# New planner durations, and a task order refined with 320 more seeds and engine pins, in a fused attention and ResMLP kernel

## The chip, the cores and the metric

The kernel runs on one core of a Trainium2 chip. The core has a matrix engine (PE, with its weight loads shown apart as PEld), a vector engine (DVE), a scalar engine (ACT), GpSimd (POOL) and a sync engine (SP), which here only issues DMAs. Each engine executes its own instructions in the order in which the program gives them, and waits on semaphores for the others. The metric is the device time of one execution in microseconds (us), the median of several runs. Beside it stands one profiled execution, whose trace gives every instruction's start and duration.

## The reference

Everything that is computed, cut to its core (B = 4 batches, 8 heads, S = 768 positions, head width 64, model width 512, hidden width 2048, 4 sink positions, a window of 128):

```python
scores = scale * q @ k.T                       # per batch and head, 768 x 768
keep = is_sink | ((rel >= 0) & (rel < window)) # 4 sinks, and the last 128 positions
a = exp(where(keep, scores, -1e9) - max); a = a / (sum(a) + 1e-9)
x = (a @ v), heads side by side                # batch, 768, 512
tok = einsum('ts,bsd->btd', w_tok, alpha1 * x + beta1)
u = x + lam * tok
ch = maximum((alpha2 * u + beta2) @ w_ch1, 0) @ w_ch2
out = u + lam * ch
```

Inputs and output are float32; the kernel multiplies in float16 and sums in float32.

## The kernel before, in words

Rows are cut into 6 tiles of 128. For each batch the stages are: load q, k and v and cast them to float16; transpose q and k (batches 0 and 1 on PE, batches 2 and 3 by a transposing DMA, L630); scores S of a key tile against two query tiles (L719 adds the mask as a bias by matmul in batch 0, L724 and L788 multiply q by k); exp on ACT into E (L746); masking of E by a multiply on DVE (L761) or two selects on POOL (L686); the sinks (L656, L661); the product with v (pv, L818 and L825) and its normalisation on DVE (L850, L851); the scaled copy xh (L860, or `mul` and `plus`, L869 and L872); mixing over tokens on PE (tok, L956), its addition on DVE (L963) and a cast (u, L356 or L358); the transpose of u (uTp on PE in batch 0, L997; a transposing DMA, L1015, afterwards); the affine step on it, uT (L980 on ACT, L982 on DVE); the first MLP product h (L1036: 512 matmuls over the four batches) with its relu (L1042 ACT, L1044 DVE); and the second MLP product. That last one is plain in batch 0 (ch, L1221). In batches 1 to 3 it is one Strassen step: seven products P1 to P7 (L1153) of sums of h halves (`h_sums`, L1094 to L1097) and differences of weight halves (`w2_sums`, L1068), added into the rows by L1166, L1184, L1189 and L1192.

The order of the work is not written by hand. Each piece is a task (`add`) with a priority, the engines on which it may run with a duration in ns for each, the tasks that it needs and the buffers that it takes. `Plan.run` simulates the five engines, the buffers and the DMA rings with these durations: again and again it takes, of the tasks that are ready, the one that can start first on the engine on which it would end first, priority breaking ties. It knows one resource that two engines share: a POOL task and a DVE task marked `port=True` never run at once in the plan. `uTx` does not mark its affine step so. A change of the PE's array shape (`mode`) costs 95 ns in the plan. `Plan.emit` then writes the instructions in the order in which the plan starts them. Before it does, it shakes the priorities: `TURNS` is a list of 30 seeds, each of which adds Gaussian noise to some priorities (`shuffle`). So the durations and the seeds settle two things and nothing else: the order of instructions in each engine's queue, and the engine of each task that has a choice. On the chip, every instruction still starts when the semaphores that it waits for allow.

Where the plan foresees that PE is idle before 36 us, it emits dummy matmuls on a zero tile (L349) that keep PE busy. They compute nothing that is used.

Buffers limit how far the order can be moved: four PSUM buffers of one bank for all products (`d`), two of two banks for the scores (`S`), six for E, twelve for the rows x, two for hT.

Of the kernel before, what the change touches and what calls it, by code (L numbers as in the profile page):

```python
# [10 lines left out]
FP16 = mybir.dt.float16  # L11
# [4 lines left out]
PE, ACT, DVE, POOL, SP = "pe", "act", "dve", "pool", "sp"  # L16
# [95 lines left out]
class Plan:  # L112
# [9 lines left out]
    def add(self, prio, engs, fn, after=(), uses=(), mode=None, lands=None, port=False,  # L122
            since=0.0):


        t = Task(len(self.tasks), prio, engs, fn, after, uses, mode, lands, port, since)
        for a in t.needs:
            a.then.append(t)
        self.tasks.append(t)
        return t  # L130

    def run(self, prio):

        tasks = self.tasks
        rank = [0] * len(tasks)
# [32 lines left out]
        def pick():  # L168
            best = None
            spare = {k: sorted(h for h, x in zip(homes[k], busy[k]) if not x) for k in homes}  # L170
            for r, i in open_:
                at = ready[i]
                if best is not None and at > best[0]:
                    continue
                t = tasks[i]
                asked = {}
                for b in t.uses:
                    if b.home is None:
                        asked[b.kind] = asked.get(b.kind, 0) + 1
                if any(len(spare[k]) < n for k, n in asked.items()):  # L180
                    continue
                at = max([at] + [spare[k][n - 1] for k, n in asked.items()])
                own = None
                for e in t.engs:
                    at_e = max(free[e], at)
                    if e == POOL or (e == DVE and t.port):
                        at_e = max(at_e, port)
                    key = (at_e + FW * t.engs[e], at_e, r, at_e + t.engs[e], i, e)
                    if own is None or key < own:
                        own = key  # L190
                if best is None or own[1:] < best:
                    best = own[1:]
            return best
# [49 lines left out]
        self.ends = free  # L243
        return steps

    def emit(self, turns):

        prio = [t.prio for t in self.tasks]
        for seed in turns:
            prio = shuffle(prio, seed)  # L250
        for t, e, start, stop, idle in self.run(prio):
            t.at = (e, start, stop)
            if idle:
                self.fill[1](self.pools["d"][0].tile(
                    [128, 512], FP32, tag=f"d_{idle[0]}", bufs=1, name=f"idle{t.i}"), idle[1])
            for b in t.uses:
                if b.t is None:
                    pool, shape, dtype = self.pools[b.kind]
                    b.t = pool.tile(b.shape or shape, b.dtype or dtype,
                                    tag=f"{b.kind}_{b.home}", bufs=1, name=b.name)  # L260
            t.fn(e)


def shuffle(prio, seed):
# [15 lines left out]
def kernel(  # L280
# [125 lines left out]
    w1f = const.tile([P, NC, DFF], FP16, name="w1f")  # L406
    w2f = const.tile([P, NF, DM], FP16, name="w2f")

    gates = sb.tile([1, 32], FP16, tag="pt_1", bufs=1, name="gates")

    STRASSEN = (1, 2, 3)
    GATES = (1, 2, 3)
# [2 lines left out]
    PAIRS = 3  # L415

    TURNS = (13523, 134113, 50022, 128275, 136711, 187603, 125671, 100730, 14946, 163131, 178432, 158827, 183776, 137680, 153375, 26742, 367527, 307353, 376563, 212018, 255075, 397706, 218147, 375675, 393913, 224567, 207692, 352780, 243076, 346008)
    W1_SINCE = 20000.0

    V0 = (((0, 1), (2, 3), (4, 5)), ((0, 1, 2), (3, 4, 5)))  # L420
# [269 lines left out]
    def scores(p, b, j, Gs, bias=False):  # L690
# [51 lines left out]
        for G, hps, n, pS, eT in units:  # L742
            done["S", b, j, G] = a

            def ex(e, n=n, pS=pS, eT=eT):
                nc.scalar.activation(  # L746
                    eT.t, pS.t[:, :, 0 : n * w].rearrange("p e (i w) -> p e i w", i=n),
                    AF.Exp, scale=scale)

            x_ = add(p + 0.1, {ACT: 170 + 2 * n * w * 0.835}, ex, [a], [pS, eT])  # L750
            if not bias:
                def mk(e, eT=eT):
                    if e == POOL:
                        ev = eT.t.rearrange("p e i w -> p (e i) w")
                        keep(ev[:, :, 0:P], 0, 1, -1)
                        if w > P:
                            keep(ev[:, :, P:w], -1, -1, 1)
                        return
                    m = mask0 if j == 0 else (maskn if j < NR - 1 else maskn[:, :, 0:P])
                    ev = eT.t.rearrange("p e i w -> p (e i) w")  # L760
                    nc.vector.tensor_mul(ev, ev, m.to_broadcast(list(ev.shape)))  # L761

                c = {DVE: 60 + 2 * n * w * 0.66}
                if b and j:
                    c[POOL] = 2 * (150 + n * w * 0.9)
                x_ = add(p + 0.2, c, mk, [x_], [eT], port=True)
            for g in (0, 1) if G is None else (G,):
                off = 2 * g if G is None else 0
                E[b, j, g] = (eT, off)
                done["E", b, j, g] = [x_]  # L770
# [38 lines left out]
    def pv(p, b, r, G):  # L809
# [46 lines left out]
        if b == 0:  # L856
            c = slice(256 * G, 256 * G + 256)

            def half(e):
                engine[e].tensor_mul(  # L860
                    bh.t[:, c], bx.t.rearrange("p h d -> p (h d)")[:, c], la1_b[:, c])

            done["xh", b, r, G] = add(
                p + 0.3, {POOL: 730}, half, [a, done["la1"]], [bx, bh], port=True)
        elif G == 1:
            bt = Buf("tm", None, None, f"tm{b}_{r}")

            def mul(e):
                engine[e].tensor_mul(bt.t, bx.t.rearrange("p h d -> p (h d)"), la1_b)  # L869

            def plus(e):
                engine[e].tensor_add(bh.t, bt.t, lb1_b)  # L872

            a = add(p + 0.3, {POOL: 1350}, mul, [a, done["x", b, r, 0], done["la1"]], [bx, bt], port=True)
            done["xh", b, r, 1] = add(
                p + 0.4, {POOL: 1390, DVE: 690}, plus, [a, done["lb1b"]] + prior, [bh, bt], port=True)
            done["xb", b, r] = None
# [55 lines left out]
    def cast_w2(p, i):  # L933
        for a in range(4 * i, 4 * i + 4):
            src = wst[f"w2_{a - a % 2}"]
            done["w2", a] = add(
                p, {DVE: 980, POOL: 1400},
                lambda e, a=a, src=src: engine[e].tensor_mul(w2f[:, a, :], src.t[:, a % 2, :], lam_b),
                [done["wst", f"w2_{a - a % 2}"], done["lam"]], [src], port=True)

# [68 lines left out]
    def uTx(p, b, ti):  # L1009

        if (b, 0) not in uT:
            uT[b, 0] = Buf("uT", None, None, f"uT{b}")
        bo, bu = uT[b, 0], u16[b, ti]
        done["uTd", b, ti] = add(
            p, {SP: 1220}, lambda e: nc.sync.dma_start_transpose(  # L1015
                bo.t[:, :, ti * P : (ti + 1) * P], bu.t),
            [done["u16", b, ti]], [bu, bo], lands=(6, 100))
        if ti % 3 < 2:
            return
        chk = ti // 3  # L1020
        for c in range(NC):
            o = (c, slice(chk * NTOK, (chk + 1) * NTOK))
            done["uT", b, chk, c] = add(
                p + 0.1 + 0.01 * c, {DVE: 380, ACT: 700},
                lambda e, c=c, o=o: affine(e, bo.t[:, o[0], o[1]], bo.t[:, o[0], o[1]], c),
                [done["uTd", b, 3 * chk + i] for i in range(3)] + [done["ab2"]], [bo])

# [29 lines left out]
    def w2_sums(p):  # L1057

        for g in range(HF // 2):
# [5 lines left out]
            def sub(o, i0, i1, after, n_):  # L1065
                def f_(e, bw=bw):
                    ab = [w2f[:, x_[0], x_[1]] if isinstance(x_, tuple) else bw.t[:, x_] for x_ in (o, i0, i1)]
                    engine[e].tensor_sub(*ab)  # L1068
                return add(p + 4 * g + n_, {DVE: 420, POOL: 1400}, f_, after, [bw], port=True)

            a1 = sub(0, (f, hi_), (f, lo_), ws, 0)
            a3 = sub((f, hi_), (k_, hi_), (f, hi_), wk + [a1] + [done.get(("ch", 0, ti)) for ti in range(NR)], 1)
# [5 lines left out]
    def h_sums(p, b, what):  # L1078
# [11 lines left out]
        for g in range(2):  # L1090
# [16 lines left out]
                after = [done["S2", b, g]] + [done["P2", b, n_] for n_ in range(3)]  # L1107
            uses = {"S3": [h0, h1, hs[g]], "S1": [h1], "S2": [h0, h1], "S4": [h0]}[what]
            uses = uses + ([own[g]] if own and what in ("S2", "S4") else [])
            done[what, b, g] = add(p + 0.1 * g, {DVE: 880}, made, after, uses, port=True)  # L1110

    hS = {}
    hS2 = {}
# [3 lines left out]
    def prod(p, b, what, nt):  # L1117
# [46 lines left out]
        def plus(p, bx, cols, more):  # L1164
            def f_(e):
                nc.vector.tensor_add(row(bx)[:, cols], row(bx)[:, cols], pc.t)  # L1166
            u_ = done["u16", b, nt if bx is top else nt + 3]
            return add(p, {DVE: 400}, f_, [a, u_] + more, [pc, bx])

        def store(p, bx, ti, cols, after):  # L1170
            n_ = (cols.stop - cols.start) // 64
# [10 lines left out]
        elif what == "P6":  # L1182
            def u2(e):
                nc.vector.tensor_add(bt.t, bt.t, pc.t)  # L1184

            u = add(p + 0.1, {DVE: 400}, u2, [a, done["read", b, "P1", nt]], [pc, bt])

            def ot(e):
                engine[e].tensor_add(row(top)[:, hi_], row(top)[:, hi_], bt.t)  # L1189
# [3 lines left out]
                    row(bot).rearrange("p (a d) -> p a d", a=2), row(bot).rearrange("p (a d) -> p a d", a=2),  # L1193
                    bt.t.unsqueeze(1).to_broadcast([P, 2, HD]))

            done["U12", b, nt] = add(p + 0.3, {POOL: 760, DVE: 400}, ot, [u, done["u16", b, nt]], [bt, top], port=True)
            done["U2", b, nt] = add(
                p + 0.2, {POOL: 1300, DVE: 690}, ob,
                [u, done["u16", b, nt + 3], done["O21", b, nt]], [bt, bot], port=True)
# [191 lines left out]
                else:  # L1391
                    pv(p, nb, *args)

    plan.emit(TURNS)


# [33 lines left out]
```

The softmax here doesn't subtract the row's maximum and nothing guards it: scores larger than these inputs give would overflow.

## Time and profile before

| what | us |
|---|---|
| median of 3 runs (lowest and highest) | 256.96 (256.52 to 257.1) |
| the profiled execution's own time | 257.06 |
| its span, first to last instruction | 255.3 |
| PE busy, of which dummy matmuls (L349, 106 of them) | 247.4, 9.4 |
| DVE, ACT, POOL busy | 190.0, 142.6, 88.3 |

The span is 1.76 us shorter than the time of its execution; what lies outside it is start and end of the program. A matmul's end is modelled in this profile: a row such as "L1036 ... x512, 326 ns mean" counts about 0.16 us after the next matmul has begun. So PE's busy time hides gaps of up to some 0.2 us, and how dense PE runs is better read from the time between the starts of matmuls. A group of the profile is one line of code on one engine with its busy time, mean duration, and the idle time of its engine just before it, with the work that ended that idle time.

### The profile page before, as it was taken

To read this page: it belongs to the slowest core of one execution; us is meant where nothing else is said; L and a number is where in the kernel's file an instruction comes from. 1 tells how busy PE (TensorE), PEld (TensorE's weight loads), DVE (VectorE), ACT (ScalarE), POOL (GpSimd) and SP (SyncE) were. 2 spreads that over 40 slices of the span, in tenths; PEclk is the share of its full clock that TensorE was granted. 3 is DMA by queue.
4 is the path that set the end of the run, shared out by engine and by line. 5 is a ranking of instruction groups with operands and counts; after the bars stand their busy time and mean duration, and the time that the engine had idled before them with its cause. 6 is when DMAs were issued, how large, how long until landed. Compare 5 with 4: busy or idle time off the path is not lost.

```text
span 255.3 us, 5519 instructions
## 1 busy us (share of the span) xinstructions
PE 247.4 (97%) x2174; PEld 160.9 (63%) x2174; DVE 190.0 (74%) x402; ACT 142.6 (56%) x236; POOL 88.3 (35%) x108
## 2 busy tenths in 40 slices
PE   8999998999999999899999999999999999999994
PEld 7754645675555544456678676558668666667883
DVE  6777998696878878578889997877789764136782
ACT  2689845989848035688971225867571125775000
POOL 7409802344445330159653460735310101000000
PEclk9999999999999999999999999999999999999999
DMA  6998999999943998599778689501000156000105
GB/s 202 195 223 292 216 230 392 373 370 218 218 73 115 186 260 190 117 205 220 155 138 182 125 191 251 85 3 21 3 0 3 59 167 146 0 0 3 63 4 185
DMA packets 86130, 38.80 MB, mean 152 GB/s; under 512 B 73540, under 2 KB 80460, under 8 KB 86104
## 3 DMA queue, kind: packets, MB, share of 16 engines
q1 hardware_dynamic: 82320, 35.14, 56.5%
q0 software_dynamic: 3744, 3.28, 8.1%
q8 instruction: 17, 0.28, 0.5%
q14 instruction: 9, 0.07, 0.1%
q10 hardware_dynamic: 40, 0.03, 0.0%
HBM read 29.91 MB, written 6.29 MB: 142 GB/s over the span
## 4 chain that ended last, share of the span: by engine, by line
PE 88%; DMA 4%; DVE 3%; POOL 1%; issue 1%; ACT 1%; POOLq 0%; ACTq 0%
PE h L1036 33%; PE P L1153 21%; PE tok L956 11%; PE ch L1221 8%; PE pv L825 5%; PE S L724 4%; DMA n<-in_q_dram 4%; DVE uT L982 1%; PE S L719 1%; PE tp L614 1%; PE pv L818 1%; POOL n L497 1%; PE wT L916 1%; ACT uT L980 1%; DVE w2f L1068 1%
## 5 line engine op out<-in xcount | busy, mean ns | idle before, releaser
L1036 PE MATMUL h<-uT,w1f 128*128 128x384 f16 x512 | 91.9, 326 | 2.7 <-DVE uT L982 1.3
L1036 PEld LDWEIGHTS <-w1f 128*128 128x128 f16 x512 | 47.3, 98 | 34.5 <-issue 5.5
L1042 ACT ACTIVATE hT<-h 128x384 f16<-128x384 f32 x99 | 48.3, 492 | 26.1 <-PE h L1036 25.6
L1153 PEld LDWEIGHTS <-hT 128*128 128x128 f16 x408 | 39.8, 98 | 6.7
L746 ACT ACTIVATE E<-S 128x1024 f16<-128x1024 f32 (+1 forms) x39 | 37.9, 1001 | 7.5 <-PE S L724 3.7
L869 POOL TENSOR_TENSOR tm<-x,la_b 128x512 f32<-128x512 f32 x18 | 26.2, 1454 | 26.3 <-DVE xh L872 19.1
L956 PE MATMUL tok<-xh,wtokT 128*128 128x512 f16 x144 | 33.4, 379 | 0.0
L356 ACT CAST u<-x 128x512 f16<-128x512 f32 x19 | 11.7, 618 | 31.2 <-DVE x L963 31.1
L1153 PE MATMUL P<-w2f,hT 128*128 128x256 f16 x216 | 25.9, 273 | 0.0
L1166 DVE TENSOR_TENSOR x<-x,P 128x256 f32<-128x256 f32 x45 | 18.3, 418 | 8.2 <-PE P L1153 7.9
L1044 DVE TENSOR_SCALAR hT<-h 128x384 f16<-128x384 f32 x29 | 15.8, 553 | 10.9 <-PE h L1036 10.5
L956 PEld LDWEIGHTS <-wtokT 128*128 128x128 f16 x144 | 14.0, 98 | 14.6
L1221 PE MATMUL ch<-w2f,hT 128*128 128x512 f16 x96 | 23.0, 379 | 0.0
L1153 PE MATMUL P<-w2s,hT 128*128 128x256 f16 x192 | 22.8, 273 | 0.0
L851 DVE TENSOR_TENSOR x<-pv,rec 128x256 f32<-128x256 f32 x48 | 20.4, 424 | 1.7
L358 POOL CAST vfs<-vnat 128x512 f16<-128x512 f32 x18 | 15.0, 840 | 16.2 <-DMA vnat<-in_v_dram 16.0
L963 DVE TENSOR_TENSOR x<-x,tok 128x512 f32<-128x512 f32 x24 | 16.2, 684 | 5.7 <-PE tok L956 5.7
L356 ACT CAST n<-nat 128x768 f16<-128x768 f32 x16 | 13.2, 829 | 10.8 <-DMA nat<-in_q_dram 8.8
L825 PEld LDWEIGHTS <-E 128*128 128x128 f16 x328 | 15.2, 97 | 6.0 <-issue 1.6
L825 PE MATMUL pv<-vfs,E 128*128 128x65 f16 x328 | 17.9, 194 | 0.0
L358 POOL CAST u<-x 128x512 f16<-128x512 f32 x5 | 3.1, 621 | 34.8 <-DVE x L963 21.1
L1221 PEld LDWEIGHTS <-hT 128*128 128x128 f16 x96 | 8.6, 98 | 9.1 <-issue 0.2
(131 smaller groups left out, 327.4 us busy)
## 6 DMA issues: line engine op xcount, KB each, us to landing
out_dram<-x SPq DMA_DIRECT2D x21, 256.0 KB, 2.8
nat<-in_q_dram SPq DMA_DIRECT2D x13, 384.0 KB, 5.3
nat<-in_k_dram SPq DMA_DIRECT2D x13, 384.0 KB, 5.7
vnat<-in_v_dram SPq DMA_DIRECT2D x18, 256.0 KB, 5.2
wst_w<-in_moe_w_ch_dram SPq DMA_DIRECT2D x8, 512.0 KB, 7.4
wtn<-in_moe_w_tok_dram SPq DMA_DIRECT2D x6, 384.0 KB, 4.7
w1f<-in_moe_w_ch_dram POOLq DMA_DIRECT2D x4, 512.0 KB, 11.1
v<-in_v_dram SPq DMA_DIRECT2D x12, 128.0 KB, 6.4
```

The source lines that it names most:

```text
L356: nc.scalar.copy(o, i)
L358: engine[e].tensor_copy(o, i)
L746: nc.scalar.activation(eT.t, pS.t[:, :, 0 : n * w].rearrange("p e (i w) -> p e i w", i=n), AF.Exp, scale=scale)
L825: nc.tensor.matmul(po.t[:, hl, :], eT.t[:, e_, off + i, c : c + P], vf[j][:, h, :], start=(r < 2 and n == 0), stop=(n == len(parts) - 1 an ...
L851: nc.vector.tensor_mul(bx.t[:, 4 * G : 4 * G + 4, :], po.t[:, :, 0:D], rec.t.to_broadcast([P, 4, D]))
L869: engine[e].tensor_mul(bt.t, bx.t.rearrange("p h d -> p (h d)"), la1_b)
L956: nc.tensor.matmul(pt.t, wtokT[:, si, ti * P : (ti + 1) * P], hs[si].t, start=(si == 0), stop=(si == NR - 1))
L1036: nc.tensor.matmul(ph.t, w1f[:, c, fi * P : (fi + 1) * P], bu.t[:, c, chk * NTOK : (chk + 1) * NTOK], start=(c == 0), stop=(c == NC - 1))
L1042: nc.scalar.activation(bh.t[:, fi, :], ph.t, AF.Relu)
L1153: nc.tensor.matmul(pc.t, hh[:, nt * P : (nt + 1) * P], w(fi), start=(first and n_ == 0), stop=(n_ == HF - 1), skip_group_check=True)
L1166: nc.vector.tensor_add(row(bx)[:, cols], row(bx)[:, cols], pc.t)
L1221: nc.tensor.matmul(pc.t, bh.t[:, fi, nt * P : (nt + 1) * P], w2f[:, fi, :], start=(fi == 0), stop=(fi == NF - 1))
```

## The change

Three things change, and all matmuls, additions, casts and DMAs stay what they are.

First, durations. Nine entries of the planner's tables get other numbers; in the order of the diff they are those of the mask of E (on POOL), tm (`mul`), the scaling of w2f (L938), the affine step uT of batches 1 to 3, `w2_sums`, `h_sums`, the additions L1166 and L1184, and U12 (L1189). Second, order. `emit` takes a second list, `NUDGES`, of 320 seeds, applied to the priorities after `TURNS`. Each seed does one of six things, chosen by a hash: move one priority, move a few, move a run of 2 to 25 neighbours together, swap two, pin one task to the first or second engine of its list (or free it), or move one and pin another. Read from the hash alone, 111 seeds swap, 108 move a run of neighbours, 57 move a few, 11 move one, 10 pin and 23 move and pin. `run` honours a pin by trying no other engine for that task. Third, the 64-byte tile `gates`, into which three tiny DMAs write so that later loads wait for the weights of h, gets its own memory; before, it shared that of the first `pt` buffer.

```diff
-    def run(self, prio):
+    def run(self, prio, pin=None):
...
-                for e in t.engs:
+                one = pin[i] if pin and pin[i] <= len(t.engs) else 0
+                for n, e in enumerate(t.engs):
+                    if one and n + 1 != one:
+                        continue
...
-    def emit(self, turns):
+    def emit(self, turns, nudges):
         prio = [t.prio for t in self.tasks]
         for seed in turns:
             prio = shuffle(prio, seed)
-        for t, e, start, stop, idle in self.run(prio):
+        pin = [0] * len(prio)
+        for seed in nudges:
+            nudge(prio, pin, seed)
+        for t, e, start, stop, idle in self.run(prio, pin):
...
+def nudge(prio, pin, seed):
+    n, x, wide = len(prio), seed, (0.5, 1, 2, 4, 8, 16, 32, 64)
...
+    kind = mix() % 6
+    w = wide[mix() % 8]
+    c = mix() % n
...
+    if kind == 0:
+        prio[c] += by()
+    elif kind == 1:
+        for _ in range(2 + mix() % 5):
+            i = (c + mix() % 60) % n
+            prio[i] += by()
+    elif kind == 2:
+        m = 2 + mix() % 24
+        y = by()
+        for i in range(c, min(c + m, n)):
+            prio[i] += y
+    elif kind == 3:
+        i = (c + 1 + mix() % 80) % n
+        prio[c], prio[i] = prio[i], prio[c]
+    elif kind == 4:
+        pin[c] = mix() % 3
+    else:
+        prio[c] += by()
+        i = (c + mix() % 30) % n
+        pin[i] = mix() % 3
...
-    gates = sb.tile([1, 32], FP16, tag="pt_1", bufs=1, name="gates")
+    gates = const.tile([1, 32], FP16, name="gates")
...
+    NUDGES = (45552149, 788903931, 542345562, 549274876,
...
-                    c[POOL] = 2 * (150 + n * w * 0.9)
+                    c[POOL] = 2 * (190 + n * w * 1.03)
...
-            a = add(p + 0.3, {POOL: 1350}, mul, [a, done["x", b, r, 0], done["la1"]], [bx, bt], port=True)
+            a = add(p + 0.3, {POOL: 1440}, mul, [a, done["x", b, r, 0], done["la1"]], [bx, bt], port=True)
...
-                p, {DVE: 980, POOL: 1400},
+                p, {DVE: 850, POOL: 1450},
...
-                p + 0.1 + 0.01 * c, {DVE: 380, ACT: 700},
+                p + 0.1 + 0.01 * c, {DVE: 450, ACT: 700},
...
-                return add(p + 4 * g + n_, {DVE: 420, POOL: 1400}, f_, after, [bw], port=True)
+                return add(p + 4 * g + n_, {DVE: 490, POOL: 1400}, f_, after, [bw], port=True)
...
-            done[what, b, g] = add(p + 0.1 * g, {DVE: 880}, made, after, uses, port=True)
+            done[what, b, g] = add(p + 0.1 * g, {DVE: 970}, made, after, uses, port=True)
...
-            return add(p, {DVE: 400}, f_, [a, u_] + more, [pc, bx])
+            return add(p, {DVE: 425}, f_, [a, u_] + more, [pc, bx])
...
-            u = add(p + 0.1, {DVE: 400}, u2, [a, done["read", b, "P1", nt]], [pc, bt])
+            u = add(p + 0.1, {DVE: 425}, u2, [a, done["read", b, "P1", nt]], [pc, bt])
...
-            done["U12", b, nt] = add(p + 0.3, {POOL: 760, DVE: 400}, ot, [u, done["u16", b, nt]], [bt, top], port=True)
+            done["U12", b, nt] = add(p + 0.3, {POOL: 1260, DVE: 425}, ot, [u, done["u16", b, nt]], [bt, top], port=True)
...
-    plan.emit(TURNS)
+    plan.emit(TURNS, NUDGES)
```

## Prediction

> **What bounds the kernel now.** I read the page's busy times first, then the table of stretches, then the chain that ended last, and then the rows of single tiles.
>
> ```profile
> PE 247.4 (97%) x2174; PEld 160.9 (63%) x2174; DVE 190.0 (74%) x402; ACT 142.6 (56%) x236; POOL 88.3 (35%) x108
> ...
> PE   8999998999999999899999999999999999999994
> PEld 7754645675555544456678676558668666667883
> ```
>
> PE is busy nearly everywhere, so PE's own work bounds the kernel, and a new order can only win back what PE loses. To see how much that is I laid the start of each matmul against the next. The dense spacings are 0.1625 us for h (in the chain, 128 in 20.80 us), 0.215 for tok (6 in 1.29) and 0.109 for P (8 in 0.87). What exceeds the dense spacing of its kind adds up to three sums: 9.7 us of dummy matmuls and what surrounds them, nearly all before 16 us; 84 changes of array shape at about 0.094, together 7.9; and 6.0 of plain stalls. The rest is matmuls that have to run, and 3.3 us between the last matmul at 252.0 and the end (the last addition and its store). The stretches say where the stalls are not:
>
> ```profile
> 38.50:41.40 2.90, 1.79 (x17) 1.03 (x16) 2.33 (x5) 1.41 (x3) 1.23 (x2) 1.00 1.05 404
> 97.00:104.00 7.00, 5.83 (x28) 2.54 (x26) 5.81 (x12) 3.39 (x6) 0.64 (x1) 1.00 0.87 189
> 104.00:130.00 26.00, 25.91 (x251) 15.57 (x249) 20.06 (x48) 22.52 (x35) 15.80 (x18) 1.00 0.87 173
> 184.00:213.00 29.00, 29.00 (x215) 20.28 (x214) 22.96 (x42) 9.56 (x18) 4.03 (x4) 1.00 0.24 64
> 213.00:233.60 20.60, 20.60 (x129) 12.44 (x128) 5.70 (x10) 15.19 (x31) 0.61 (x1) 1.00 0.11 27
> ```
>
> The columns are the stretch, its length, and the busy us of PE, PEld, DVE, ACT and POOL. After 184 us PE has no gap; by the spacings, the whole of 184 to 252 loses under 0.1 us. The losses sit at two joints, where the h of a batch begins. The chain shows both:
>
> ```profile
> 39.06 0.68 ACT uT L980
> 39.76 0.87 DVE uT L982 x2
> 40.66 0.68 ACT uT L980
> 41.38 2.27 PE h L1036 x13
> ...
> 97.91 0.69 DVE x L1232
> 98.60 1.34 DVE w2f L1068 x4
> 99.94 1.26 DVE x L963 x2
> ...
> 102.78 0.59 DVE uT L982
> 103.41 1.91 PE h L1036 x10
> ```
>
> At 39 us, PE has finished tok and the transposes of u, and the four affine steps run one after another on ACT and DVE; PE issues 3 h matmuls (0.49 us) in 2.30 us, from 39.08 to 41.38: 1.8 lost. At 101.38 PE's last tok is out; DVE had put a row addition (0.69) and four weight differences (1.34) ahead of the tok additions on which uT waits, and dense h begins only at 103.41: 1.6 lost. Two smaller stalls follow at 110.8 (0.25) and 179.6 (0.53). These four are 4.2 of the 6.0.
>
> **What the Trainium skill says.** Its page Perfetto Trace Analysis, section Identifying the Most-Contended Engine, warns that matmul busy time is a poor measure of nearness to the limit, because matmuls are pipelined; the trace agrees, with 97% beside 63% of weight loads and a mean of 326 ns against a spacing of 162.5. TensorE: Matmul & The Clock Gate, section Back-to-back issue gap, gives N / 2.4 + 2.5 ns for an isolated matmul, 162.5 for 384 columns, just the spacing seen; its lower figure for a stream of 512 columns (131 ns) is not what this trace shows (215). SBUF — State Buffer, section SBUF: two separate sides, says that DVE and POOL share a pair of ports under an exclusive lock, the loser blocked for a whole instruction. The trace agrees:
>
> ```profile
> L982 DVE TENSOR_SCALAR uT<-uT,ab x17: 365/376/1424, 102.4 to 218.3; 128x384 f16<-128x384 f16 x17
> L869 POOL TENSOR_TENSOR tm<-x,la_b x18: 1260/1272/1917, 71.5 to 186.2; 128x512 f32<-128x512 f32 x18
> L1189 POOL TENSOR_TENSOR x<-x,pt x3: 1171/1231/1372, 146.3 to 198.6; 128x256 f32<-128x256 f32 x3
> ```
>
> These are least, median and longest ns. A uT of 376 took 1424 once, at 177.9 us, under an xh of POOL (1.27 us), and that was the stall at 179.6.
>
> **The change, part by part.** (1) Durations. None is work; a cost matters only through the order and engines it leads to. Most move towards the means of the page: tm 1350 to 1440 (mean 1454), U12 on POOL 760 to 1260 (1258), h sums 880 to 970 (23.5 us over 24: 979), L1166 400 to 425 (418), w2 on DVE 980 to 850 (735), uT 380 to 450 (502). The worst error mended is U12: three of nine went to POOL at 1.26 us where DVE takes 0.42. Moved to DVE they add 1.3 us to an engine with idle time in those stretches (22.96 busy of 29.00 at 184 to 213): 0 us, between −0.5 and +0.3 if the cover is gone, since each then delays one release of a PSUM buffer by 0.42.
>
> (2) Joint at 97 to 103. The four weight differences (L1068, 0.418 each by its row, slightly overlapped) hold 1.34 us of the chain. P7 of batch 1 needs them first, at 135 us, so they can go behind the tok additions. What is late next is the transposing DMA of u (median 2.4 us from issue to landing), which ran beside them. I take −1.3, between −1.6 (all) and 0.
>
> (3) Joint at 38 to 41. Some tok work, 1.29 us a tile, can stand between the transposes of u and h, as it needs only xh. Then the affine steps run under it: −1.3 of 1.8, between −1.8 and 0. POOL's and ACT's casts of u (0.61) must then not come later than the second half of h needs, which has 5 us.
>
> (4) Small stalls: −0.25 of the 0.78, between −0.8 and 0.
>
> (5) Start and shapes. The first loads bind the start (the chain waits for a q load from 6.03 to 15.40), so the dummies are cover for it; I take −0.2, between −1.5 and +1. Of 84 shape changes, pairing scores with scores saves two each time, 0.19; I take −0.2, between −1.0 and +0.5.
>
> (6) What the plan still does not know: uT is not marked for the port. A new place for it meets a POOL instruction as it meets one now. One such meeting costs 1.424 − 0.376 = 1.05 us; I add one, between 0 and four.
>
> (7) `gates`: three DMAs of SP into own memory. The first user of the old memory is a `pt` at 131 us or later, the last gate DMA issues at 44.8: 0 us either way.
>
> (8) The pins: 33 seeds pin, so at most 33 tasks. A mask moved from DVE to POOL costs 2 × 0.634 for 0.73; it is inside (6).
>
> Sum: −1.3 −1.3 −0.25 −0.2 −0.2 +1.05 = −2.2 us. The profiled execution, 255.3 of span and 1.76 around it, 257.06, becomes 254.9; its 0.1 above the median taken off, 254.8.
>
> **Rivals.** A, gain does not carry over: the plan closes its own gaps, while on the chip transfers and the port move them elsewhere. For it: the order before also stems from such a plan, and 6 us of stalls remain. Against: 3.4 of the 6 are plain queue order, visible to durations that fit the trace within some 15%. Time 257.0, give or take 0.5.
>
> B, all of it: both joints closed (−3.4), the small stalls (−0.8), start and shapes −1.0, no new meeting: −5.2, 251.8. For it: DVE (74%), ACT (56%) and POOL (35%) have room. Against: the start hangs on loads.
>
> C, slower, by one mechanism: the port at the joints. The place is the start of h in batches 1, 2 and 3 (now about 101, 158 and 213 us), where uT needs DVE within 2 to 4 us of the last tok. If the new order stretches POOL's xh and tm chain, with more masks on POOL, over these places, each of the six chunks of uT (24 affine steps in all) adds up to 1.05 us on PE's path. The gain of 3.25 (items 2 to 5) is used up at three meetings; five give +2.0, 259.0. For it: POOL's busy stretches (15.80 of 26.00 at 104 to 130) lie beside h, and the plan cannot see the meeting. Against: before, 16 of 17 uT ran undisturbed or nearly so.
>
> D, no change of order: excluded in practice, as 320 seeds move most priorities by more than the spacing of 0.5 between neighbours.
>
> **How the numbers follow.** The forecast (−3.5 to −0.5) gets 0.42, B (beyond −3.5) 0.18, A (within 0.5) 0.14, C 0.26. Within 0.2% (0.5 us) is about what a measurement of this kernel cannot tell from no change. So faster 0.60, same 0.14, slower 0.26. The forecast's own range is 253.5 to 256.4. Eight in ten: 252.0 leaves out half of B (0.08), 259.0 the worse half of C (0.12). Signs are mixed, but one side holds most.
>
> **What would show it.** Right: h at the first joint dense within 1 us of the last transpose; no L1068 in the chain near 98 us; PE stalls of 3 to 4 us in all; after 130 us no new gap. Joint (3) right but (2) wrong: first h of batch 1 still 1.5 us behind tok. Item (6): a uT over 1 us long just ahead of a late h. C: several of those, or L686 and L869 in the chain. Item (5): the first tok moved from 30.4 us by more than 0.5. The prediction is wrong if the last 120 us, now dense, get gaps, since no item above prices any there.

## The result: 263.7 us, slower, and the profile after

| what | before | after |
|---|---|---|
| median, us (lowest and highest of 4 runs each, the runs before repeated beside those after) | 256.77 (256.52 to 257.1) | 263.7 (262.2 to 264.2) |
| ratio, 95% interval | | 1.026 (1.021 to 1.031) |
| profiled execution, us; its span | 257.06; 255.3 | 264.2; 262.4 |
| TensorE clock granted over the span | 0.999 | 0.992 |

The new order costs 6.9 us. (Each ratio here and below rests on the fast runs alone; this leaves out one run of d6, at 262.65 us.) The prediction, 254.8 with a range up to 259.0, is missed. Lines after the change are about 52 higher than before: h is L1088, tok L1008, the addition of tok L1015, the scores S L776, the sinks L708, the affine step uT L1032 (ACT) and L1034 (DVE), the sums of h halves hS L1146, P L1205. The transposing DMAs are L682 (q and k) and L1067 (u).

The page of the kernel after, with its busy times and two rows of the 40 slices:

```profile
PE 249.1 (95%) x2173; PEld 161.4 (61%) x2173; DVE 195.2 (74%) x403; ACT 139.4 (53%) x228; POOL 95.0 (36%) x114
...
PE   8989998999999996599999999999979999999994
...
PEclk9999999999999999799999999999999999999999
```

PE executes as many matmuls as before (2173 records beside 2174). Two places are new: a 6, a 5 and, in the clock's row, a 7 at about 100 to 112 us, and a 7 at about 193 us, in the stretch that was dense before. A table of PE's waits (us in total, times, longest) names both:

```profile
PE S L776 <- DMA qkT<-n: 5.0, 1, 5.0
PE P L1205 <- DVE hS L1146: 1.4, 1, 1.4
```

One wait of 5.0 us, of scores S for a transposing DMA, is nearly all of it. The stretches around it (from:to, length, busy us and count of PE, PEld, DVE, ACT, POOL, then the granted clock, the busy share of the DMA engines and GB/s):

```profile
94.00:102.50 8.50, 8.50 (x42) 3.72 (x40) 6.78 (x16) 3.70 (x6) 0.00 (x0) 1.00 1.17 244
102.50:107.70 5.20, 0.27 (x3) 0.08 (x2) 2.24 (x5) 2.30 (x4) 0.61 (x1) 1.00 0.67 132
107.70:112.00 4.30, 4.27 (x22) 1.95 (x23) 1.60 (x3) 2.83 (x5) 1.48 (x2) 0.60 1.16 218
```

PE is all but empty for 5.2 us, and in the 4.3 us after that it is full but at a mean clock of 0.60. In these, seven h matmuls start 320 ns apart and the two around them 292 and 240, instead of 162.5: 1.3 us more. The sinks just ahead of them cost another 0.2. The Trainium skill's TensorE: Matmul & The Clock Gate, section What's actually happening, says that the array falls to half its clock after an idle window of some 3.4 us and returns after about as long a busy one. The trace agrees: 320 is close to twice 162.5, and a mean of 0.60 over 4.30 us is what some 3.4 us at half clock and the rest at full clock give (an estimate from these two numbers).

From the spacings of matmul starts, as the prediction counted them, the 7.1 us between the two spans are made up so:

| where | loss before | loss after | difference |
|---|---|---|---|
| up to the first dense h (41.38, then 41.84 us) | | | 0.5 |
| 97 to 104 us before, 97 to 109 after: stall | 1.6 | 5.1 | 3.5 |
| up to 130 us, the slow clock in it | 0.6 | 1.7 | 1.1 |
| 174 to 200 us | 0.6 | 1.7 | 1.1 |
| the rest, by difference (small stalls, end, one more shape change: 85, not 84) | | | 0.9 |

The first row belongs to this execution and not to the order. It is the slowest of the four (264.2; the fastest took 262.2). In the executions of d2 to d7 below, whose order is the same up to there, dense h begins at 40.6 to 41.1 us, and in p1 and p2, which have the old order there, at 41.0. The stall is long in it, too: d4, which leaves the joint alone, has 3.7 us.

**How the 5 us arise.** The chain that ended last, at this joint (start, duration, what; the steps of under 0.1 us between them left out):

```profile
98.71 0.70 DVE x L1015
...
99.43 0.63 ACT u L407
100.06 0.80 SPq L682
...
100.96 3.12 DMA uT<-u
...
104.18 0.62 ACT u L407
...
104.89 2.79 DMA qkT<-n
...
107.73 0.56 PE S L776 x6
...
108.84 4.01 PE h L1088 x16
```

The tok that the chain follows ends at 98.69 and its addition on DVE at 99.41. The cast of u is followed by SP's queue (L682, a transpose of k), then by three transposes of u, then by one more transpose of k, and the scores of batch 2 that wait for it stand on PE ahead of h. SP issues DMAs one after another; its rows in the timeline after:

```profile
92.23 3.23 SPq L682 DMA_TRANSPOSE qkT<-n  x1
...
98.09 0.44 SPq L560 DMA_DIRECT2D nat<-in_k_dram  x1
98.62 0.78 SPq L1287 DMA_DIRECT2D out_dram<-x  x1
99.49 1.36 SPq L682 DMA_TRANSPOSE qkT<-n  x1
100.96 3.84 SPq L1067 DMA_TRANSPOSE uT<-u  x3
104.89 1.24 SPq L682 DMA_TRANSPOSE qkT<-n  x1
```

And before:

```profile
95.97 4.02 SPq L1015 DMA_TRANSPOSE uT<-u  x3
100.08 0.53 SPq L1235 DMA_DIRECT2D out_dram<-x  x1
100.71 2.60 SPq L630 DMA_TRANSPOSE qkT<-n  x2
```

The three transposes of u now come 5.0 us later, and three queues share in that. The first addition of tok starts 1.7 us later (96.12 for 94.46), since PE comes to the tok of batch 1 later. The cast after it loses another 1.0 on ACT, behind the cast of a k tile. From the end of the cast (98.43) to the issue of its transpose SP takes 2.5 us, where it took 0.2 before (95.80 to 95.97). So the last affine step of uT ends only at 107.07 us, and S, ahead of h on PE, waits until 107.73.

**The second place.** The timeline at 192 us (start, duration, engine, line, operation, output and inputs, count, and in brackets the idle time before it with what ended it):

```profile
191.87 1.27 POOL L924 TENSOR_TENSOR xh<-tm,lb_b 128x512 f16<-128x512 f32 x1
...
192.13 3.77 DVE L1146 TENSOR_TENSOR hS<-hT,hT 128x1536 f16<-128x1536 f16 x2
193.22 1.87 POOL L921 TENSOR_TENSOR tm<-x,la_b 128x512 f32<-128x512 f32 x1
...
195.96 1.05 PE L1205 MATMUL P<-w2f,hS 128*128 128x256 f16 x8 [1.35 <-DVE hS L1146]
```

Two sums hS, 0.95 us each elsewhere, take 3.77 us beside two instructions of POOL that are each on the shared port, and P7 waits for them. The planner keeps POOL and a marked DVE task apart, but only in its own times: in the plan POOL's xh begins as the second hS ends, on the chip it began 0.26 us ahead of the first, and nothing holds it back.

### The profile page after: what moved, and what is told of

Same layout as the page of the kernel before. It is cut to its first block, busy times and chain, and to the rows that moved or that the text cites. A ratio compares the mean times of both kernels' runs of the same rounds, so it can differ in the third digit from the quotient of the medians.

```text
span 262.4 us, 5503 instructions
## 1 busy us (share of the span) xinstructions
PE 249.1 (95%) x2173; PEld 161.4 (61%) x2173; DVE 195.2 (74%) x403; ACT 139.4 (53%) x228; POOL 95.0 (36%) x114
## 4 chain that ended last, share of the span: by engine, by line
PE 85%; DMA 6%; DVE 5%; POOL 1%; issue 1%; ACT 1%; SPq 0%; POOLq 0%; ACTq 0%; DVEq 0%
PE h L1088 32%; PE P L1205 19%; PE tok L1008 10%; PE ch L1273 8%; PE pv L877 4%; PE S L776 4%; DMA n<-in_q_dram 3%; DVE hS L1146 1%; PE S L771 1%; DMA uT<-u 1%; DMA qkT<-n 1%; PE tp L666 1%; PE pv L870 1%; DVE hT L1147 1%; POOL n L549 1%
## 5 line engine op out<-in xcount | busy, mean ns | idle before, releaser
L1088 PE MATMUL h<-uT,w1f 128*128 128x384 f16 x512 | 91.5, 329 | 0.7 <-ACT uT L1032 0.4
L1088 PEld LDWEIGHTS <-w1f 128*128 128x128 f16 x512 | 48.3, 99 | 33.2 <-issue 5.2
L1094 ACT ACTIVATE hT<-h 128x384 f16<-128x384 f32 x90 | 43.9, 490 | 27.4 <-PE h L1088 26.8
L1205 PEld LDWEIGHTS <-hT 128*128 128x128 f16 x408 | 39.8, 98 | 6.7 <-issue 0.5
L921 POOL TENSOR_TENSOR tm<-x,la_b 128x512 f32<-128x512 f32 x18 | 25.2, 1402 | 24.2 <-DVE xh L924 16.8
L1008 PE MATMUL tok<-xh,wtokT 128*128 128x512 f16 x144 | 32.2, 379 | 0.0
L1096 DVE TENSOR_SCALAR hT<-h 128x384 f16<-128x384 f32 x38 | 20.8, 554 | 13.6 <-PE h L1088 13.0
L1205 PE MATMUL P<-w2f,hT 128*128 128x256 f16 x216 | 26.8, 272 | 0.1
L1008 PEld LDWEIGHTS <-wtokT 128*128 128x128 f16 x144 | 14.0, 98 | 15.7
L1205 PE MATMUL P<-w2s,hT 128*128 128x256 f16 x192 | 23.4, 273 | 0.1
L1241 POOL TENSOR_TENSOR x<-x,pt 128x256 f32<-128x256 f32 x3 | 2.7, 895 | 54.0 <-DVE pt L1236 54.0
L1015 DVE TENSOR_TENSOR x<-x,tok 128x512 f32<-128x512 f32 x24 | 16.1, 683 | 3.2 <-PE tok L1008 2.9
L776 PE MATMUL S<-qkT 64*128 64x256 f16 (+1 forms) x156 | 12.7, 270 | 5.0 <-DMA qkT<-n 5.0
L877 PE MATMUL pv<-vfs,E 128*128 128x65 f16 x328 | 16.9, 193 | 0.0
```

The lines of the kernel that those rows point to most:

```text
L776: nc.tensor.matmul(pv_[:, e_, i, :], o.t[rows, 2 * hp + 1, j * P : (j + 1) * P], o.t[rows, 2 * hp, j * P : j * P + w], start=not bias, sto ...
L877: nc.tensor.matmul(po.t[:, hl, :], eT.t[:, e_, off + i, c : c + P], vf[j][:, h, :], start=(r < 2 and n == 0), stop=(n == len(parts) - 1 an ...
L1008: nc.tensor.matmul(pt.t, wtokT[:, si, ti * P : (ti + 1) * P], hs[si].t, start=(si == 0), stop=(si == NR - 1))
L1088: nc.tensor.matmul(ph.t, w1f[:, c, fi * P : (fi + 1) * P], bu.t[:, c, chk * NTOK : (chk + 1) * NTOK], start=(c == 0), stop=(c == NC - 1))
L1094: nc.scalar.activation(bh.t[:, fi, :], ph.t, AF.Relu)
L1096: nc.vector.tensor_scalar_max(bh.t[:, fi, :], ph.t, 0.0)
```

## Experiments

All build on the kernel's own task list. Two lists were added to `emit`: `plan.moves` takes a task out of the written order and puts it right behind another one, and `plan.to` gives a task another engine. (A third, `plan.warm`, serves d5 alone.) Every other instruction keeps its place in its queue. The d experiments edit the kernel after, the p experiments the kernel before. Ratios are against the kernel before, measured on the same chip.

```diff
-        for t, e, start, stop, idle in self.run(prio, pin):
+        steps = self.run(prio, pin)
+        for t, e in self.to:
+            steps = [(s[0], e) + s[2:] if s[0] is t else s for s in steps]
+        for t, a in self.moves:
+            s = [s for s in steps if s[0] is t]
+            steps = [s_ for s_ in steps if s_[0] is not t]
+            n = [s_[0] for s_ in steps].index(a) + 1
+            steps[n:n] = s
+        for t, e, start, stop, idle in steps:
```

### d1: the durations alone

```diff
-    plan.emit(TURNS, NUDGES)
+    plan.emit(TURNS, ())
```

> The new durations with the 30 old seeds alone, no further seeds and no pins. Theory 1 (the order is what counts, and the old seeds were good only together with the old durations): the order is dealt anew and is poor, 263 to 268 us, as slow as the changed kernel or slower. Rival (the 320 seeds and pins do the harm, the durations are closer to the trace and do none): 255 to 258 us, about the time before.

Measured: 263.1 us (262.2 to 264.8), ratio 1.024 (1.020 to 1.029); span 260.5. PE's waits:

```profile
PE S L776 <- DMA qkT<-n: 2.6, 1, 2.6
PE pv L877 <- DVE hT L1096: 1.4, 1, 1.4
```

The nine durations alone (with the new memory of `gates`, which this run has too) cost all that the change costs. The same joint stalls, for 2.6 us, and a wait of pv that neither other kernel has comes to it; the clock is 1.0 in this execution and 0.993 in the other three. The 320 seeds then bought nothing on the chip (263.1 to 263.7, within each other's runs). The planner's own numbers fit this. Each kernel computes a planned start for every task; these are the kernel's own numbers and no measurement. Its plan ends at 252.9 us before, 263.0 with the new durations alone and 252.2 after the seeds. So the seeds won back 10.8 planned us, and all that the plan promised against the kernel before was 0.6, counted with two different sets of durations. The plan also has a stall at the joint: before the first scores of batch 2 PE stands for 3.2 planned us, where the plan of the kernel before has 2.1 ahead of h. So the search did not overlook this stall; it accepted it, and the chip made it longer.

### d2: h ahead of the scores on PE

```diff
+    row_ = [h_[8], done["h", 1, 0, 8], sc_, sk_, x0, es_, x1]
+    plan.moves += list(zip(row_[1:], row_[:-1]))
+    plan.moves += [(done["h", 1, 0, 0], done["h", 1, 0, 15]), (m0, x1)]
```

`h_` are the first three groups of h of batch 1, with their relus `done["h", ...]`; `sc_`, `sk_`, `x0`, `x1`, `es_`, `m0` are the first scores of batch 2, their sinks, exps and mask.

> The changed kernel; on PE, at the joint of batch 0 and 1, three groups of h now stand ahead of the scores of batch 2 and their sinks (exps and masks follow). Nothing else moves. Theory 1 (the step uT is late too, because its casts and transposes stand behind q and k work in the queues of ACT and SP): h can start about 106.9 instead of 107.7 us, so 0.9 us less and perhaps 0.5 us from the clock, 262 to 263 us. Rival (the stall is PE's order alone, scores put ahead of h that was ready): 5 us and the clock's 1.4 us come back, 257 to 258 us.

Measured: 263.22 us (260.46 to 263.3), ratio 1.021 (1.016 to 1.027). Stretches of this kernel, columns as above:

```profile
101.30:105.30 4.00, 0.45 (x3) 0.10 (x1) 1.50 (x3) 1.70 (x4) 0.61 (x1) 1.00 0.64 124
105.30:109.00 3.70, 3.48 (x12) 1.41 (x11) 1.86 (x5) 0.89 (x3) 0.28 (x1) 0.62 0.99 201
```

PE now waits 3.9 us for uT in place of the scores, until 105.52, and the slow clock follows all the same in this execution. (Three of the four runs have a clock of 0.993; the fourth, with 260.46 us, has 1.0.) So the place of S on PE, though it is what the profile of the kernel after names, is not the cause by itself: u is late too.

### d3: u ahead of q and k in every queue

```diff
+    (the lines of d2, and:)
+    plan.moves += [(c31, u_[2]), (t31, d_[2])]
+    plan.moves += [(stores[0], t11), (stores[1], stores[0])]
+    plan.moves += [(done["u", 1, 4], a_[3]), (done["u16", 1, 4], done["u", 1, 4])]
```

On ACT the cast of k tile (3,1) goes behind the casts of u; on SP its transpose goes behind the transposes of u, and two stores behind the last transpose of k; on DVE the addition of the fifth tok goes behind the affine steps.

> As the run with h ahead of the scores, and also: ACT casts u of row tiles 1, 0 and 2 ahead of the cast of a k tile of batch 2, SP issues the three transposes of u ahead of the transpose of that k tile and of two output stores, and DVE does the affine steps ahead of the addition of row tile 4. Theory 1: h starts near 104.3 us, the idle time of PE falls from 5.1 to under 2 us, the clock stays up: 4 to 5 us less than the changed kernel, 258.5 to 260 us. Rival (PE's order alone): no better than the run without these moves.

Measured: 260.09 us (260.02 to 260.58), ratio 1.012 (1.010 to 1.015): 3.6 us of the 6.9 are back. PE's longest wait:

```profile
PE h L1097 <- DVE uT L1043: 1.6, 2, 1.4
```

The stretch, columns as above:

```profile
100.90:104.00 3.10, 1.34 (x7) 0.58 (x6) 2.24 (x5) 1.71 (x3) 0.07 (x1) 1.00 0.68 132
```

The gap of 5.1 us has become two of 1.57 and 0.52, and the clock is 1.0 throughout. P's wait for hS at 192 us (1.3 us in this kernel's waits) is untouched, as it should be. The order in the queues that feed uT is thus the cause of most of the joint's stall, and the slow clock is its consequence. Four queues were changed at once, and their shares were not tried one by one. The traces say that SP's is the largest: in d2, before the affine steps, DVE and ACT both stand idle (2.0 and 1.5 us) until a transpose of u lands, and the first one was issued 2.8 us after its cast had ended; in d3 it is 0.7. The moves also make a new wait, 0.8 us of pv for a masking on DVE, and PE comes to tok no earlier than in the kernel after.

### d7: one transpose of k behind the loads on SP

```diff
+    plan.moves += [(t01, done["nat", 2, 3, 1])]
```

> The changed kernel with one move on SP: the transposing DMA of a k tile of batch 2 (issued at 87 us, landed 6.0 us later where 2.8 is usual) stands behind the next q and k loads instead of ahead of them. Theory (this transpose among loads is what makes the two loads land 2 us later than the plan has it, and the casts on ACT with them): the casts come about 2 us earlier and 1.5 to 2.5 us come back, 261 to 262 us. Rival (the loads are as late behind any order, since the queue of SP is full here): 263 to 264 us.

Measured: 263.21 us (262.94 to 265.19), ratio 1.026 (1.022 to 1.031). The casts of the two late tiles of q and k came 3.9 and 3.8 us earlier (91.04 and 93.32 us instead of 94.97 and 97.07, some 0.8 of it because this execution began earlier), yet the transposes of u were still issued only at 99.06, and PE stood for 4.0 us. The cast of u no longer waits behind that of k: it ended at 96.67, and its transpose was issued 2.4 us later. d4 shows the same (96.45 and 98.55). So the late loads are not needed for the stall; they are worth at most the 1.1 us by which it is shorter here. The time does not show even that, since the slow clock lasts longer: eleven h matmuls start 320 ns apart, seven in the kernel after.

### d4: no POOL work on the port at 192 us

```diff
+    late = done["xh", 3, 4, 1]
+    plan.to += [(late, DVE)]
+    plan.moves += [(late, done["S3", 2, 1])]
```

> The changed kernel, with one addition of xh (batch 3, row tile 4) moved from POOL to DVE, behind the two hS. Theory 1 (the hS at 192 us takes 3.77 us for two instead of 1.94 because POOL's addition holds the shared port, and P7 on PE waits 1.4 us for it): hS back to under 1 us each, the gap of PE at 194.3 gone, 1.3 to 1.6 us less than the changed kernel, about 262.1 us. Rival (hS is late for another reason, such as the relus that it reads): hS as long or late as before, no change.

Measured: 260.65 us (260.26 to 262.18), ratio 1.015 (1.011 to 1.019). DVE's rows of the timeline in that place:

```profile
189.82 0.95 DVE L1155 TENSOR_TENSOR hS<-hT,hT 128x1536 f16<-128x1536 f16 x1
190.69 0.68 DVE L933 TENSOR_TENSOR xh<-tm,lb_b 128x512 f16<-128x512 f32 x1
191.29 0.95 DVE L1155 TENSOR_TENSOR hS<-hT,hT 128x1536 f16<-128x1536 f16 x1
```

Both hS take 0.95 again, even with the xh between them on DVE, and the gap of PE went from 1.5 us to 0.16. That shows the port meeting. The time fell by 3.05 us, more than the gap is worth: in this profile the joint stalls for 3.7 us instead of 5.1 and the start is about 1 us earlier, neither of which the edit touches. d6 below gives the cleaner price.

### d5: dummy matmuls in the stall

```diff
+    plan.warm[sc_] = (sk_.uses[1], 80)
```

Eighty matmuls of 128 columns on the zero tile are put ahead of the scores of batch 2 on PE, into the PSUM buffer that the sinks overwrite next. Nothing of them is used.

> The changed kernel with 80 dummy matmuls (4.5 us at 56 ns) ahead of the scores of batch 2 that wait for the q and k transposes, where PE stands idle for 3.7 to 5.1 us. All work is there; the dummies compute nothing used. Theory 1 (the idle time makes the chip grant PE a lower clock for the next 3 to 4 us, and ten h matmuls then take 320 ns instead of 163): the clock stays at 1.0 and 1.4 to 1.6 us come back, about 262.2 us. Rival (the slow h matmuls have another reason, or the dummies delay the scores as much as they save): no change, 263.7 us.

Measured: 261.1 us (260.85 to 261.74), ratio 1.018 (1.016 to 1.020). The dummies in the chain, and the stretch after them:

```profile
101.52 4.47 PE sk L415 x80
```

```profile
108.00:112.00 4.00, 4.00 (x34) 2.42 (x33) 3.36 (x8) 3.49 (x5) 2.18 (x3) 1.00 1.04 154
```

The dummies fill the stall from the last tok to the scores at 105.99, and the clock stays at 1.0 (0.998 to 1.0 in all four runs). Useless work makes the kernel 2.6 us faster than the kernel after. Of this, 1.5 is what the slow matmuls and sinks had lost; the stall was also 0.6 shorter in this execution (4.47 beside 5.1), which nothing in the edit explains. The remaining 0.5 is open.

### d6: d3 and d4 together

> The changed kernel with u first in the queues of ACT, SP, DVE and PE at the joint of batch 0 and 1, and the addition of xh at 192 us on DVE. Theory 1 (two separate causes, which add): 3.6 of the first and 1.4 of the second, 258.5 to 259 us, still above the time before, the rest being the start and small stalls. Rival (the second stall only absorbs what the first delays): no better than the first repair alone, 260.1 us.

Measured: 258.49 us (258.18 to 259.51, three runs; with the run of 262.65, whose clock was 0.993, the median is 259.0), ratio 1.008 (1.006 to 1.011); span 256.5, clock 1.0. That is 1.6 us less than d3 by these medians and 1.1 by the ratios; the table has 1.1 for the stretch of the port meeting. Two places thus hold about two thirds of the loss, the joint with its clock 3.6 us and the port 1.1 to 1.6, together 4.7 to 5.2 of 6.9. The rest is not pinned down. The largest waits left are again at h of batch 1 (1.1 us behind DVE's uT, 0.7 behind ACT's), where the affine steps stand behind a tok addition and a cast of u; p2's kind of move was not tried there. Even with both repaired, the new order is not faster than the old one.

### p1 and p2: the prediction's step (2), done by hand in the kernel before

```diff
+    plan.moves += [(done["T3", g], a_[3]) for g in (0, 3, 2, 1)]          # p1
+    plan.moves += [(done["u", 1, 5], a_[3]),
+                   (done["u16", 1, 5], done["u", 1, 5])]                  # p2 has both
```

In p1 the four weight differences go behind the affine steps of batch 1. In p2 the addition and cast of the last tok go there too.

> The kernel before, with its old order, and the four weight differences T3 on DVE moved from ahead of the tok additions of batch 1 to behind the affine steps. The prediction's step for this joint: 1.3 us less, 255.6 us. Reading the chain again after the result: the affine steps on DVE also stand behind the addition of the last tok (from 101.8 us), and the transposes of u land at 101.2, so moving the differences alone gives 0 to 0.3 us, 256.6 to 256.9.

> As the run with the weight differences moved, and the addition of the last tok of batch 1 moved behind the affine steps too. If transposes that land at 101.2 us are what remains, h is dense near 102.4 instead of 103.4: 0.8 to 1.0 us less than before, about 256.0 us. If something else holds h, no change.

Measured: p1 256.64 us, ratio 1.0003 (0.9993 to 1.0013); p2 256.02 us, ratio 0.998 (0.9965 to 0.999). The differences are gone from p1's chain, and dense h of batch 1 begins at 103.06 us instead of 103.41; but the h of batch 0 is 0.36 us earlier in this execution already. DVE's rows show why nothing came of it. The kernel before:

```profile
101.80 0.69 DVE L963 TENSOR_TENSOR x<-x,tok 128x512 f32<-128x512 f32 x1 [0.61 <-PE tok L956]
102.40 1.24 DVE L982 TENSOR_SCALAR uT<-uT,ab 128x384 f16<-128x384 f16 x3
```

p1, then p2:

```profile
101.44 0.69 DVE L972 TENSOR_TENSOR x<-x,tok 128x512 f32<-128x512 f32 x1 [0.61 <-PE tok L965]
102.05 1.25 DVE L991 TENSOR_SCALAR uT<-uT,ab 128x384 f16<-128x384 f16 x3
```

```profile
100.71 0.96 DVE L991 TENSOR_SCALAR uT<-uT,ab 128x384 f16<-128x384 f16 x3
```

In the kernel before, already, DVE stood idle for 0.61 us after the weight differences, until PE had finished the last tok. So the differences held up nothing that uT waits for. What held uT was the addition of that tok, which stands ahead of the affine steps. In p2 it stands behind them, and they start at 100.71 us; so the transposes of u had landed by then, and it was not they that held uT in p1. Step (2) as it was put is worth nothing. With the last addition out of the way as well, 0.6 us come back, and h then waits 0.62 us for the affine step on ACT, which stands behind a cast of u.

### p3: the prediction's step (3) by hand

```diff
+    plan.moves += [(done["tok", 0, 3], done["uT", 0, 0, 3].needs[0])]
+    plan.moves += [(done["u", 0, 3], done["uT", 0, 0, 3]),
+                   (done["u16", 0, 3], done["u", 0, 3])]
```

One tok tile of batch 0 goes between the transposes of u and h on PE, its addition and cast behind the affine steps.

> The kernel before, with its old order, and the tok of row tile 3 (batch 0) moved on PE behind the transposes of u, its addition and cast behind the affine steps. The prediction's step for the joint at 38 to 41 us: 1.3 us of the 1.8 come back, 255.4 us; worked out again from the queue of DVE, h is dense about 40.4 instead of 41.4 us: 0.9 less, 255.8 us. Rival (h waits for something else at that point, such as the weights of h): no change, 256.7 us.

Measured: 256.31 us (22 runs), ratio 0.998 (0.997 to 0.9993): 0.46 us. The move does what was said, at a third of the price: h then waits 1.04 us for DVE instead, which has the displaced addition to do.

### p4: p2, p3 and the port meeting at 178 us of the kernel before

```diff
+    (the lines of p2 and p3, and:)
+    late = done["xh", 3, 2, 1]
+    plan.to += [(late, DVE)]
+    plan.moves += [(late, done["uT", 2, 1, 2])]
```

> The kernel before with the two moves at the joint near 100 us (0.6 us measured), the tok moved behind the transposes of u, and the POOL addition of xh that holds the port at 177 us moved to DVE behind the affine steps (0.5 us by the stall that follows it). If the repairs are independent: 0.6 + 0.9 + 0.5 = 2.0 us less than before, 254.7 us. Rival (a repair only moves the wait on to the next late thing): 255.5 to 256.1 us.

Measured: 255.11 us (254.93 to 255.84, 6 runs; before 256.77, 27 runs), ratio 0.993 (0.990 to 0.995); span 253.3. This is faster than both kernels. Its chain at 177 us, where PE lost 0.53 before:

```profile
177.34 0.98 PE P L1162 x8
178.32 0.65 PE h L1045 x4
```

Only PE is left in it: no uT of 1.42 us holds h back. At the joint of batch 1 dense h begins at 101.63 us, 1.8 earlier than before. So there was a gain of 1.7 us in the places that the prediction named, and the old durations with three groups of moves by hand reach it.

## Why the prediction was wrong, by its own steps

**Step (1), durations at 0 us, failed first.** It priced each duration by the engine it would move work to. d1 shows that they redeal the whole order: +6 us with nothing else changed but the memory of `gates`. That better numbers lead to a better order was taken for granted. Nor did the example come true: three U12 are still on POOL in the kernel after.

```profile
L1241 POOL TENSOR_TENSOR x<-x,pt x3: 727/729/1229, 212.0 to 256.2; 128x256 f32<-128x256 f32 x3
```

The trace of before had 1171 ns at the least. The 1260 that the plan was given belonged to one order, not to the operation. The two traces show what goes with the difference: the four that took 1171 ns or more all run beside a DVE instruction that reads two SBUF tiles (`x<-x,pt`, or one of the sums of h halves), the two of 727 and 729 only beside additions that read PSUM (`x<-x,P`). If the port is the reason, the 1260 already held a meeting that the plan believes it avoids; no run varies this alone.

**Step (2), −1.3 at 97 to 103 us, failed in sign.** It failed on the kernel before, to begin with: the chain names the four weight differences, but DVE's rows have 0.61 us of idle time behind them, and p1 shows that they were worth 0. The step said itself what would be late next, the transposing DMA of u, but took it at its usual 2.4 us from issue to landing and gave its queue no price. In the kernel after, u's transposes stand behind others on SP and their casts behind another on ACT, and the place went from 1.6 us of stall to 5.1. d3 shows the queues as the cause. A cost that no step had is the clock after an idle PE, 1.5 us by the spacing of the slow matmuls. The range's lower bound on the gain of this place was 0; a new order can also lose there.

**Step (3), −1.3 at 38 to 41 us.** Done by hand, in p3, the move works and gives 0.46. The size was off by a factor of three, because the displaced addition comes back on DVE's queue. The kernel after does not make this move: all its tok ends before the transposes of u (at 39.62). Its stall did fall, from 1.8 to 1.2 us, but because two affine steps run back to back on ACT (40.56 to 41.80) where a pair on DVE stood between them. A gain at this place was forecast rightly, by another road than the one that was taken.

**Steps (4) and (5).** The stall at 179.6 is gone in the kernel after, worth 0.5; the table has it in the row of 174 to 200 us, under the new stall there. Shape changes are 85 instead of 84, and the start differs more between executions of one order than the 0.2 that was forecast for it. Both steps were small.

**Step (6), one more meeting on the port, +1.05.** Right in kind: the gap of PE at hS is 1.5 us, and 1.1 net of the stall at 179.6 that is gone; d6 has 1.1 to 1.6. That this is close to 1.05 is luck, since that figure was the lengthening of one uT. The wrong operation was named: the longest uT now takes 0.82 us instead of 1.42, and the meeting is that of hS, which the plan does know:

```profile
L1034 DVE TENSOR_SCALAR uT<-uT,ab x13: 366/375/820, 106.1 to 225.3; 128x384 f16<-128x384 f16 x13
L1146 DVE TENSOR_TENSOR hS<-hT,hT x6: 949/957/2021, 133.9 to 242.8; 128x1536 f16<-128x1536 f16 x6
```

(Least, median and longest ns of a tile, in the kernel after.) The page of the Trainium skill that the prediction quoted, SBUF — State Buffer, section SBUF: two separate sides, speaks of exactly this lock, and the trace agrees for hS as it did for uT: 2021 beside 949. Marking a task for the port in the plan does not keep it off the port on the chip. (The prediction's example needs a correction: the uT of 1424 ns began at 178.39 us, when the xh of POOL had just ended and a tm had begun, at 178.43.)

**Steps (7) and (8)** were not tried alone. No wait of the profile after leads to `gates`.

**The rivals.** C, the slower one, had the right place, the start of h in batch 1, and the wrong cause; it asked for five port meetings at uT, and one that PE waited for came, elsewhere. What the prediction held against C was misread: not one of the 17 uT before was disturbed but five, with 552 to 1424 ns beside a median of 376. A said that the plan closes its own gaps while on the chip transfers and the port move them elsewhere. That is the nearest to what happened, though at the joint the plan left itself a gap of 3.2 us. A's price was a zero sum within 0.5 us, and nothing bounds the sum at zero. The rows that it would have needed are the issue times of SP's transposes, where the order before has u first. The sign that the prediction gave for its own failure, gaps in the last 120 us, did appear (at 194 us), and was the smaller part.

## What to carry to other kernels

A search over orders improves the order in its own model, and so it also finds what the model gets wrong: here late DMAs in queues that go in order, a clock that falls when PE has been idle, and a port that nothing enforces. Before trusting such an order, lay the planned start of each queue's instructions beside the trace, and ask of every in-order queue what stands ahead of the transfer that the next stage needs. Here the plan of the kernel after has the first addition of tok in batch 1 at 95.0 us and the first transpose of u at 96.9; the trace has them at 96.1 and 101.0. PE's work was 1.1 us late by then, SP's 4.1. A few moves made by hand, at the stalls that a trace shows and in all the queues that feed them, gained 1.7 us where the renewed search lost 6.9.

## What was not expected of the hardware

- A transposing DMA can hold its issuing queue for long. Most take SP 1.2 to 1.4 us each; right behind a load one took 3.23 us (at 92.23, shown above), and the load ahead of it 3.13 us.
- At 90 to 92 us of the kernel after, the DMA engines were busy (share 1.24; packets count with their whole time in the stretch in which they begin) and moved only 25 GB/s, where the kernel before moved 219 GB/s at a share of 0.81. In that time a transpose issued at 86.99 took 6.0 us to land, against a median of 2.8 here. The hole is there in several other executions too, weaker in d4 and d6. Its cause is open.
- An idle PE costs more than its idle time. After 3.7, 3.9 and 5.1 us (d4, d2, after) the next stretch ran at a clock of 0.60 to 0.62; after 2.6 us (d1's profiled execution) and gaps of 1.57 and 0.52 us (d3), or with dummies in the stall (d5), it ran at 1.0. It is not the same in every execution: one of the four runs of d2 kept a clock of 1.0.
- The duration of one operation in a trace is not fixed: the addition U12 on POOL took 1.17 to 1.37 us in the order before and 0.73 for two of three in the order after, which met no DVE instruction with two inputs in SBUF.
